# Operands of single-pass float32 matmuls moved to fixed places within 512 bytes of on-chip memory

## The chip, the cores and the metric

One core of one Trainium2 chip runs the whole kernel as one program. The metric is device time in microseconds, the median of several executions. TensorE (PE) multiplies: for each matmul it first loads a 128x128 block of weights (an instruction of its own, PEld in the profile) and then streams the columns of the other operand, the moving one, past it. VectorE (DVE), ScalarE (ACT) and GpSimd (POOL) do the rest, SyncE (SP) issues most transfers. On-chip memory has 128 partitions; an operand of a matmul lies at one byte address, the same in all partitions.

## The reference

Three parts in a row, on 8 sequences of 3072 tokens of width 256, in float32.

```
X = rfft(x, axis=1)
Yr = Xr @ w_r - Xi @ w_i + b_r;  Yi = Xr @ w_i + Xi @ w_r + b_i
Yr, Yi = sign(Y) * max(|Y| - 0.01, 0)        # each
x = irfft(Yr + i Yi)                         # 24576 x 256
# experts, top 1 of 8, where x @ w_skip > 0:
x = x + gate * (relu(x @ w1[e]) @ w2[e])     # 256 -> 1024 -> 256
# feed forward
h = max(x @ w1, x @ w2, x @ w3);  out = h @ w_out   # 256 -> 768 -> 256
```

## The kernel before

To keep float32's accuracy with single-pass matmuls (the type `fp32r`), the kernel splits an operand in two: a high part (ACT's copy into `fp32r`) and a low part (the rest, by DVE or POOL), and sums three products: high by high, high by low and low by high. So each product of the three parts is a group of three matmuls, or of a multiple of three. Some small products of the Fourier steps are plain `fp32`, which the profile shows as two passes each.

**Spectral stage** (`spectral`), one batch after the other, the order written out by hand. The Fourier transform is done in two steps forward (`f1_mm`, L264; `f2`, L281) and two back (`if2`, L345; `if1`, L359). In between `wmm` (L316) multiplies by `w_r` and `w_i`: its weights (the operand that stays in PE) are the data, `xh` and `xl` from pool `fst`, its moving operands the split matrices `wrh`, `wrl`, `wih`, `wil`. For a batch there are 12 steps with two frequency groups each: 8 passes of L281, 24 matmuls of L316, 6 of L345 (11 of the 12 steps). In L345 the constants `ic2h`, `ic2l` are the weights and `yh`, `yl` move. Then `to_rows` (L370) brings the tokens back into rows and multiplies by the gate, and `gating` writes each token to a row of its expert by an indirect DMA.

**Expert stage** (`experts`): a loop over tiles of 256 tokens of one expert, 52 of them here. In an iteration 48 matmuls of L910 make the hidden layer (weights `w1h`, `w1l`, moving `xh`, `xl`, 256 columns) and 48 of L933 the output (weights `hh`, `hl`, moving `w2h`, `w2l`, 256 columns). The tiles' table (`hot`, `q`, `tab`) is worked out on DVE ahead of the loop from `grid`, a constant that counts up, which is loaded at the kernel's start and kept.

**Feed-forward stage** (`feed_forward`): 24 blocks of 1024 tokens, nine units each; a unit is one of three weight matrices at one of three column pairs, as a Strassen-like product of seven half-size products (`product`, L1048: weights `wu`, moving `xh`, `xl`, 512 columns, three matmuls each). After each third unit the outputs of an earlier one (`outputs`, L1126: weights `wo`, moving `hh`, `hl`, 512 columns) are dealt into the units, four matmuls at a time. Products go to PSUM tiles `pa`, `pb`, `pc`; ACT copies some (`keep`, L1055), DVE adds others (`add`, L1058), takes the maximum (L1093, L1094) and prepares the next block (`prepare`, L986 to L1007). `pb` and `pc` have one buffer each, so the next product into `pb` waits for DVE's addition to have read the last.

**Where tiles lie.** A pool (`tc.tile_pool`) is a stretch of memory. Left-hand pools are stacked upwards in the order in which they are opened, right-hand ones (`side="right"`) downwards from the end, and each tile takes the next bytes in its pool in the order of its first request, rounded up to 32. `keep` is the first left-hand pool; the first pool of each stage (`fcst`, `mcst`, `wst`) begins where it ends. On the right lie the constants and `g2` of the spectral stage (`fec`), its input (`fx`), and after the last batch the feed-forward stage's weights (`fw`).

Of the kernel before, what the change touches and what calls it, by code (L numbers as in the profile page):

```python
# [10 lines left out]
F32 = mybir.dt.float32  # L11
F32R = mybir.dt.float32r
# [10 lines left out]
E = 8  # L23
FF = 1024
F2D = 768
LAM = 0.01
TM = 256
# [3 lines left out]
NBLK = S // 128  # L31
NTMAX = NT // TM + E + 2
WO = 9 * 7 * 128
WL = WO + 6 * 256
WHY = "every count is bounded by the number of tokens"


# [75 lines left out]
@with_exitstack  # L113
def kernel(ctx: ExitStack, tc: tile.TileContext, ins, out: bass.AP):
    nc = tc.nc
    G = E + 1

    dram = ctx.enter_context(tc.tile_pool(name="dram", bufs=1, space=bass.MemoryType.DRAM))
    rows = dram.tile([E * CAP, RW], F32, name="rows")
    xt = dram.tile([NT, D], F32, name="xt")  # L120
    wsc = dram.tile([2, 128, WL], F32, name="wsc")

    keep = ctx.enter_context(tc.tile_pool(name="keep", bufs=1))
    ident = keep.tile([128, 128], F32, name="ident")
    make_identity(nc, ident)
    base = keep.tile([128, G], F32, name="base")
    small = keep.tile([128, 64], F32, name="small")
    nc.sync.dma_start(out=small, in_=ins["c_small"])

    def split(src, h, l, act=True):  # L130
        if act:
            nc.scalar.activation(out=h, in_=src, func=AF.Copy)
        else:
            nc.vector.tensor_copy(out=h, in_=src)
        nc.vector.tensor_tensor(out=l, in0=src, in1=h.bitcast(F32), op=ALU.subtract)

    grid = keep.tile([E, NTMAX], F32, name="grid")
    nc.gpsimd.dma_start(out=grid, in_=ins["c_tile"])

    fw = {}  # L140

    def feed_weights():
        pool = ctx.enter_context(tc.tile_pool(name="fw", bufs=1, side="right", reuse_waits="tile"))
        fw["pool"] = pool
        fw["wo"] = [pool.tile([128, 6, D], F32R, name=f"wo{i}") for i in range(2)]
        for i in range(2):
            nc.sync.dma_start(
                out=fw["wo"][i].rearrange("p c d -> p (c d)").bitcast(F32), in_=wsc[i, :, WO:WL]
            )
            yield  # L150
        for u in range(2):
            load_unit(u)
            yield

    def load_unit(u):
        t = fw["pool"].tile([128, 2, 896], F32R, tag="wu", name="wu", bufs=3)
        at = 896 * (u % 9)
        nc.sync.dma_start(
            out=t.bitcast(F32), in_=wsc[:, :, at:at + 896].rearrange("w p f -> p w f")
        )  # L160
        fw[u] = t

    spectral(tc, ins, rows, xt, wsc, base, small, ident, split, feed_weights(), G)
    experts(tc, ins, rows, xt, base, small, grid, ident, split, G)
    feed_forward(tc, xt, fw, load_unit, out)


def spectral(tc, ins, rows, xo, wsc, base, small, ident, split, feed, G):
    nc = tc.nc
    x = ins["x"]  # L170
    with ExitStack() as ctx, ExitStack() as early:
        cst = ctx.enter_context(tc.tile_pool(name="fcst", bufs=1))
        ec = early.enter_context(tc.tile_pool(name="fec", bufs=1, side="right"))
        xp = early.enter_context(tc.tile_pool(name="fx", bufs=4, side="right"))
        big = ctx.enter_context(tc.tile_pool(name="fbig", bufs=5))
        zp = ctx.enter_context(tc.tile_pool(name="fz", bufs=3))
        st = ctx.enter_context(tc.tile_pool(name="fst", bufs=2))
        gp = ctx.enter_context(tc.tile_pool(name="fg", bufs=1))
        ps = ctx.enter_context(tc.tile_pool(name="fps", bufs=2, space=bass.MemoryType.PSUM))

        yk = cst.tile([128, NBLK, CW], F32, name="yk")
        f1 = cst.tile([N1, 128], F32, name="f1")
        c2 = ec.tile([128, NF, 128], F32, name="c2")
        ic2h = ec.tile([128, NF, 128], F32R, name="ic2h")
        ic2l = ec.tile([128, NF, 128], F32R, name="ic2l")
        ic2 = ec.tile([128, 2, 128], F32, name="ic2")
        ic1 = cst.tile([128, N1], F32, name="ic1")
        tri = cst.tile([128, 128], F32, name="tri")
        bt = cst.tile([NBLK // 2 * G, 2, (NBLK + 1) * G], F32, name="bt")
# [1 line left out]
        ones = cst.tile([128, 128], F32, name="ones")  # L191
        bias = cst.tile([128, 256], F32, name="bias")
        bias0 = cst.tile([128, 256], F32, name="bias0")
        wrh = cst.tile([128, 2, 256], F32R, name="wrh")
        wrl = cst.tile([128, 2, 256], F32R, name="wrl")
        wih = cst.tile([128, 2, 256], F32R, name="wih")
        wil = cst.tile([128, 2, 256], F32R, name="wil")
        tok = cst.tile([128, NBLK], F32, name="tok")
        pad = yk[:, 0:1, 0:RW]
        nc.gpsimd.memset(pad, 0.0)  # L200
        nc.gpsimd.memset(pad[:, :, 257:258], 1e6)
# [9 lines left out]
        with tc.manual_schedule():  # L211
# [6 lines left out]

            warm(9)
            nc.sync.dma_start(out=f1, in_=ins["c_f1"])  # L220
            wr = st.tile([128, 2, 256], F32, tag="v", name="wr", bufs=1)
            wi = st.tile([128, 2, 256], F32, tag="c", name="wi", bufs=1)

            ic2f = zp.tile([128, 32, 128], F32, tag="z", name="ic2f")

# [6 lines left out]
            xt = load_x(0, range(4))  # L232
            for h, o in enumerate((0, CW - G)):
# [3 lines left out]
                    out=gi[:, o + E:o + G], in_=ins["moe_w_skip"][sl].rearrange("(p o) -> p o", o=1)  # L237
# [345 lines left out]
            g2 = f1_all(0, xt)  # L583
# [14 lines left out]
            for b in range(B):  # L598
                nxt = b + 1 < B
                if b == 0:  # L600
                    for e in range(E):
                        a = nc.sync.dma_start(
                            out=rows[CAP * e:CAP * e + TM].rearrange("(p s) c -> p s c", s=2),
                            in_=pad.to_broadcast([128, 2, RW]),
                        )
                        tc.add_to_no_dep_group("dispatched", a.ins)
                if nxt:
                    xt = load_x(b + 1, range(4))
# [120 lines left out]
                if nxt:  # L729
                    g2 = g2n  # L730
# [1 line left out]
                pass  # L732


def experts(tc, ins, rows, xo, base, small, grid, ident, split, G):
    nc = tc.nc
    w1d, w2d = ins["moe_w1"], ins["moe_w2"]
    with ExitStack() as ctx:
        cst = ctx.enter_context(tc.tile_pool(name="mcst", bufs=1, reuse_waits="tile"))
        st = ctx.enter_context(tc.tile_pool(name="mst", bufs=1, reuse_waits="tile"))  # L740
# [2 lines left out]

        w2h = cst.tile([128, 8, D], F32R, name="w2h")
        w2l = cst.tile([128, 8, D], F32R, name="w2l")
        hh = cst.tile([128, 8, TM], F32R, name="hh")
        hl = cst.tile([128, 8, TM], F32R, name="hl")
        xs = cst.tile([128, 8, 64], F32, name="xs")
        xt = cst.tile([128, 2, TM], F32, name="xt")
        xr = cst.tile([128, 2, RW], F32, name="xr")  # L750
        xh = cst.tile([128, 2, TM], F32R, name="xh")
        xl = cst.tile([128, 2, TM], F32R, name="xl")
        idx = cst.tile([128, 2], I32, name="idx")
        zero = cst.tile([128, 2], I32, name="zero")
        w1f = cst.tile([128, 2, FF], F32, name="w1f")
        w2f = cst.tile([128, 8, D], F32, name="w2f")
        w1h = cst.tile([128, 2, FF], F32R, name="w1h")
        w1l = cst.tile([128, 2, FF], F32R, name="w1l")

        def value(ap, hi, engines=None):  # L760
            kw = {} if engines is None else {"engines": engines}
            return nc.values_load(ap, min_val=0, max_val=hi, skip_runtime_bounds_check_because=WHY, **kw)

# [34 lines left out]
        with tc.manual_schedule():  # L798
# [12 lines left out]
                out=ti, in0=base[0:E, 0:E], scalar=float(TM - 1), in1=at, op0=ALU.add, op1=ALU.subtract  # L811
# [3 lines left out]
            for i, d in enumerate((1, 2, 4)):  # L815
                nc.vector.tensor_tensor(
                    out=sums[:, i + 1, 4:12], in0=sums[:, i, 4:12], in1=sums[:, i, 4 - d:12 - d], op=ALU.add
# [4 lines left out]
                out=most[:, 0, 4:12], in0=sums[:, 3, 3:11], scalar=1.0, in1=has, op0=ALU.add, op1=ALU.mult  # L822
            )
            for i, d in enumerate((1, 2, 4)):
                nc.vector.tensor_tensor(
                    out=most[:, i + 1, 4:12], in0=most[:, i, 4:12], in1=most[:, i, 4 - d:12 - d], op=ALU.max
# [4 lines left out]
                out=has[0:1], in0=most[0:1, 3, 4:12], scalar1=0.0, scalar2=None, op0=ALU.is_equal  # L831
# [10 lines left out]
                out=top, in0=base[0:E, 0:E], scalar1=-float(TM), scalar2=None, op0=ALU.add  # L842
# [4 lines left out]
                out=v, in0=v, in1=ident[0:E, 0:E].unsqueeze(1).to_broadcast([E, 6, E]), op=ALU.mult  # L847
# [11 lines left out]
                out=q[:, 0], in0=grid, scalar1=float(TM), scalar2=o, op0=ALU.mult, op1=ALU.add  # L859
            )  # L860
            nc.vector.scalar_tensor_tensor(
                out=q[:, 0], in0=q[:, 0], scalar=top, in1=hot, op0=ALU.min, op1=ALU.mult
# [3 lines left out]
                out=q[:, 2], in0=grid, scalar1=1.0, scalar2=starts, op0=ALU.add, op1=ALU.is_equal  # L866
# [14 lines left out]
            for j, copy in enumerate((nc.scalar.copy, nc.vector.tensor_copy)):  # L881
                copy(
                    out=v[:, j].rearrange("p k (q c) -> p k q c", q=4),
                    in_=xr[:, j, 0:D].rearrange("p (q k c) -> p k q c", q=4, k=2),
# [7 lines left out]
        with tc.manual_schedule(), tc.For_i(0, nt, 1, iteration_sync="reg_based") as t:  # L892
# [3 lines left out]
            for c in range(4):  # L896
# [8 lines left out]
                for j in range(2):  # L905
                    f0 = 128 * (2 * c + j)
                    i = 0
# [9 lines left out]
                    out=hl[:, sl], in0=p, scalar=0.0, in1=hh[:, sl].bitcast(F32), op0=ALU.max, op1=ALU.subtract  # L917
# [10 lines left out]
            for j in range(2):  # L928
                y = py.tile([128, D], F32, name="y_ps")
                i = 0  # L930
                for c in range(8):
                    for a, v in ((hh, w2h), (hl, w2h), (hh, w2l)):
# [5 lines left out]
                    out=ob[:, j], in0=y, scalar=xr[:, j, 256:257], in1=xr[:, j, 0:256],  # L938
# [3 lines left out]
                    out=seen[:, j], in0=ob[:, j, 0:1], in1=ob[:, j, 1:2], op=ALU.add  # L942
# [3 lines left out]
                        out=xo[:, :],  # L946
                        out_offset=bass.IndirectOffsetOnAxis(ap=idx[:, j:j + 1], axis=0),
                        in_=ob[:, j],
# [285 lines left out]
```

## Time and profile before

| | us |
|---|---|
| median of 3 runs | 2979.63 (2975.47 to 2982.6) |
| the profiled execution's own time | 2972.22 |
| its span, first to last instruction | 2970.5 |
| mean granted clock of TensorE | 0.987 |

The span is shorter than the execution's time by what lies around it. The profile's busy times say how long an engine had something in it; matmuls overlap, so that the sum of their durations says little, and the starts in the timeline say how many a stretch took. [...] Times in the timeline are from the span's start.

### The profile page before, as it was taken

Reading aid. Unit: us, or ns where it says so; the run is one execution under the profiler, and the core shown is the slowest. Engines: PE = TensorE matmul, PEld = TensorE weight load, DVE = VectorE, ACT = ScalarE, POOL = GpSimd, SP = SyncE. Lnnn points to the kernel's source line nnn. Section 1 sums busy time; section 2 is a strip of 40 time slices with the busy share of each in tenths; the row PEclk is TensorE's granted clock in tenths of the full one; section 3 lists DMA queues with packets and bytes.
Section 4 is the critical chain, followed back from the end, with each engine's and each line's share of the span. In section 5 each row is a group of like instructions: output and inputs, shape, how many; then the busy total and the mean of one; then the engine's idle time right before and its main releaser. Section 6 shows DMA issues by size and latency. Waiting matters only on the chain.

```text
span 2970.5 us, 53442 instructions
## 1 busy us (share of the span) xinstructions
PE 2876.5 (97%) x17158; PEld 2492.8 (84%) x17159; DVE 1835.7 (62%) x2707; ACT 1374.1 (46%) x2657; POOL 1224.4 (41%) x1206
## 2 busy tenths in 40 slices
PE   9999999999969999999699999999999999999998
PEld 8889988898969999999577777777777777777776
DVE  6877777766545455544466665666656666666664
ACT  4444544454423333333255555555555555555553
POOL 2033223222432222222255555555555555555554
PEclk9999999999979999999899999999999999999999
DMA  5323333332343333333356555665556655566543
GB/s 154 123 89 106 103 108 93 110 98 89 102 131 103 96 100 102 94 103 93 92 161 179 165 163 157 177 179 165 163 157 177 179 165 163 157 177 179 165 149 105
DMA packets 400157, 398.83 MB, mean 134 GB/s; under 512 B 272634, under 2 KB 318279, under 8 KB 399988
## 3 DMA queue, kind: packets, MB, share of 16 engines
q1 hardware_dynamic: 385428, 369.80, 44.4%
q0 software_dynamic: 14560, 26.86, 2.6%
q8 instruction: 97, 1.59, 0.2%
q14 instruction: 72, 0.59, 0.1%
HBM read 307.69 MB, written 101.91 MB: 138 GB/s over the span
## 4 chain that ended last, share of the span: by engine, by line
PE 45%; DVE 3%; ACT 1%; issue 1%; DMA 0%; SPq 0%; POOL 0%; DVEq 0%
PE pa L1048 19%; PE o_ps L1126 12%; PE pb L1048 10%; PE pc L1048 5%; DVE m L1094 2%; ACT hh L1105 1%; DVE xl L1007 1%; DVE m L1058 0%; ACT xh L1004 0%; DVE xc L986 0%; DMA xs<-xt 0%; SPq L980 0%; POOL hl L1106 0%; DVE xt L991 0%; DVE t L1058 0%
## 5 line engine op out<-in xcount | busy, mean ns | idle before, releaser
L1048 PE MATMUL pa<-xh,wu 128*128 128x512 f32 x1728 | 616.4, 397 | 19.9 <-ACT xh L1004 19.6
L1055 ACT ACTIVATE s<-pa 128x512 f32<-128x512 f32 x648 | 379.2, 596 | 338.1 <-PE pa L1048 215.1
L1106 POOL TENSOR_TENSOR hl<-m,hh 128x512 fp32r<-128x512 f32 x288 | 398.3, 1405 | 301.5 <-ACT hh L1105 301.5
L1048 PEld LDWEIGHTS pa<-xh,wu 128*128 128x128 f32 x1728 | 325.8, 189 | 99.9 <-ACT xh L1004 19.8
L1048 PE MATMUL pb<-xh,wu 128*128 128x512 f32 x864 | 347.9, 403 | 7.6 <-DVE m L1058 5.9
L1048 PE MATMUL pa<-xl,wu 128*128 128x512 f32 x864 | 342.8, 397 | 3.5 <-DVE xl L1007 3.5
L1126 PE MATMUL o_ps<-hh,wo 128*128 128x512 f32 x1152 | 340.7, 398 | 3.4 <-ACT hh L1105 3.4
L1085 POOL TENSOR_TENSOR t<-s,s 128x512 f32<-128x512 f32 x144 | 186.9, 1298 | 268.3 <-ACT s L1055 268.3
L1126 PEld LDWEIGHTS o_ps<-hh,wo 128*128 128x128 f32 x1152 | 217.5, 189 | 57.3 <-ACT hh L1105 4.7
L915 ACT ACTIVATE hh<-h_ps 128x512 fp32r<-128x512 f32 x208 | 120.6, 597 | 299.5 <-PE h_ps L910 283.7
L1055 ACT ACTIVATE s<-pb 128x512 f32<-128x512 f32 x216 | 129.4, 599 | 272.2 <-PE pb L1048 272.0
L1094 DVE TENSOR_TENSOR m<-m,t 128x1536 f32<-128x1536 f32 x144 | 251.8, 1748 | 0.0
L916 DVE SCALAR_TENSOR_TENSOR hl<-h_ps,hh 128x512 fp32r<-128x512 f32 x208 | 139.4, 689 | 174.6 <-ACT hh L915 143.0
L933 PE MATMUL y_ps<-w2l,hh 128*128 128x256 f32 x832 | 236.2, 284 | 1.0 <-POOL w2l L778 0.4
L933 PE MATMUL y_ps<-w2h,hl 128*128 128x256 f32 x832 | 235.4, 283 | 0.0
L933 PE MATMUL y_ps<-w2h,hh 128*128 128x256 f32 x832 | 235.3, 283 | 0.0
L469 POOL DMA_INDIRECT rows<-yk,pos x192 | 195.3, 1017 | 91.9 <-issue 60.9
L910 PE MATMUL h_ps<-xh,w1h 128*128 128x256 f32 x832 | 230.1, 277 | 1.6 <-DVEq L892 1.6
L910 PE MATMUL h_ps<-xl,w1h 128*128 128x256 f32 x832 | 230.1, 277 | 0.0
L910 PE MATMUL h_ps<-xh,w1l 128*128 128x256 f32 x832 | 229.8, 276 | 0.0
L1048 PEld LDWEIGHTS pb<-xh,wu 128*128 128x128 f32 x864 | 162.8, 188 | 65.2 <-DVE m L1058 15.9
L1105 ACT ACTIVATE hh<-m 128x512 fp32r<-128x512 f32 x288 | 165.7, 626 | 81.4 <-DVE m L1094 81.4
(248 smaller groups left out, 6989.2 us busy)
## 6 DMA issues: line engine op xcount, KB each, us to landing
wu<-wsc SPq DMA_DIRECT2D x216, 896.0 KB
xc<-in_x_dram SPq DMA_DIRECT2D x64, 384.0 KB
xt<-yk SPq DMA_DIRECT2D x192, 128.0 KB
xs<-xt SPq DMA_DIRECT2D x192, 128.0 KB
out_dram<-ob SPq DMA_DIRECT2D x192, 128.0 KB
xr<-rows SPq DMA_DIRECT2D x53, 264.0 KB
xs<-rows SPq DMA_DIRECT2D x208, 64.0 KB, 2.3
w1f<-in_moe_w_dram SPq DMA_DIRECT2D x9, 1024.0 KB
```

What stands on the lines that cost most here:

```text
L469: a = nc.gpsimd.indirect_dma_start(out=rows[:, :], out_offset=bass.IndirectOffsetOnAxis(ap=pos, axis=0), in_=yk[:, t, G:G + RW], in_offset ...
L910: nc.tensor.matmul(p[:, j], lhsT=a[:, k, f0:f0 + 128], rhs=v[:, k], start=(i == 0), stop=(i == 5))
L915: nc.scalar.activation(out=hh[:, sl], in_=p, func=AF.Relu)
L916: nc.vector.scalar_tensor_tensor(out=hl[:, sl], in0=p, scalar=0.0, in1=hh[:, sl].bitcast(F32), op0=ALU.max, op1=ALU.subtract)
L933: nc.tensor.matmul(y, lhsT=a[:, c, 128 * j:128 * j + 128], rhs=v[:, c], start=(i == 0), stop=(i == 23))
L1048: nc.tensor.matmul(o, lhsT=self.w[:, g, at:at + 128], rhs=v[h], start=(start and i == 0), stop=(i == 2), skip_group_check=True,)
L1055: nc.scalar.activation(out=self.s[k], in_=o, func=AF.Copy)
L1085: nc.gpsimd.tensor_tensor(out=self.t[:, 2], in0=self.s[5], in1=self.s[7], op=ALU.add)
L1094: nc.vector.tensor_tensor(out=m[:, 0:3], in0=m[:, 0:3], in1=self.t, op=ALU.max)
L1105: nc.scalar.activation(out=hh[:, i], in_=m[:, i], func=AF.Copy)
L1106: nc.gpsimd.tensor_tensor(out=hl[:, i], in0=m[:, i], in1=hh[:, i].bitcast(F32), op=ALU.subtract)
L1126: nc.tensor.matmul(o, lhsT=wo[g][:, 2 * p + c, 128 * k:128 * k + 128], rhs=h[v][:, (0, 3, 1, 2)[2 * t + c]], start=(p == 0 and i == 0), st ...
```

## The change

Nothing that is computed, no order of matmuls and no shape is changed; tiles are requested in another order, unused tiles (`spacer`) are put between, and one constant moves from one pool to another. `spacer(pool, n)` requests n float32 values per partition, 4n bytes, that nobody uses.

```diff
+def spacer(pool, n, i=0):
+    pool.tile([128, n], F32, name=f"spacer{i}", bufs=1)
...
-    grid = keep.tile([E, NTMAX], F32, name="grid")
-    nc.gpsimd.dma_start(out=grid, in_=ins["c_tile"])
...
     (feed_weights, after wo0, wo1 and the first two wu)
+        spacer(pool, 120)
...
     (spectral)
+        st = ctx.enter_context(tc.tile_pool(name="fst", bufs=2))
         big = ctx.enter_context(tc.tile_pool(name="fbig", bufs=5))
         zp = ctx.enter_context(tc.tile_pool(name="fz", bufs=3))
-        st = ctx.enter_context(tc.tile_pool(name="fst", bufs=2))
...
+        wrh = cst.tile([128, 2, 256], F32R, name="wrh")
+        wrl, wih, wil likewise, now the first tiles of cst
         yk = cst.tile([128, NBLK, CW], F32, name="yk")
...
+        ec.tile([128, 16, 256, 2], F32, tag="g2", name="g2")
+        spacer(ec, 120)
...
-        tok = cst.tile([128, NBLK], F32, name="tok")
+        tok = gp.tile([128, NBLK], F32, name="tok")
...
+            spacer(st, 16)
             wr = st.tile([128, 2, 256], F32, tag="v", name="wr", bufs=1)
             wi = st.tile([128, 2, 256], F32, tag="c", name="wi", bufs=1)
+            for t in ("yh", "yl"):
+                st.tile([128, 2, 256], F32R, tag=t, name=t, bufs=1)
+            spacer(st, 16, 1)
...
     (experts)
         w2h = cst.tile([128, 8, D], F32R, name="w2h")
         w2l = cst.tile([128, 8, D], F32R, name="w2l")
+        xh = cst.tile([128, 2, TM], F32R, name="xh")
+        xl = cst.tile([128, 2, TM], F32R, name="xl")
+        spacer(cst, 16)
         hh = cst.tile([128, 8, TM], F32R, name="hh")
         hl = cst.tile([128, 8, TM], F32R, name="hl")
+        w1h = cst.tile([128, 2, FF], F32R, name="w1h")
+        w1l = cst.tile([128, 2, FF], F32R, name="w1l")
         xs = cst.tile([128, 8, 64], F32, name="xs")
         xt = cst.tile([128, 2, TM], F32, name="xt")
         xr = cst.tile([128, 2, RW], F32, name="xr")
-        xh, xl, and further down w1h, w1l from their old places
...
+        grid = cst.tile([E, NTMAX], F32, name="grid")
+        nc.sync.dma_start(out=grid, in_=ins["c_tile"])
```

## Rows read from the trace of the kernel before

**Rows 1.** The page, part 1: engine, busy us, share of the span, instructions.
```profile
PE 2876.5 (97%) x17158; PEld 2492.8 (84%) x17159; DVE 1835.7 (62%) x2707; ACT 1374.1 (46%) x2657; POOL 1224.4 (41%) x1206
```

**Rows 2.** Windows by stage: stretch, its length, busy us (instructions) per engine, clock, DMA.
```profile
0.00:856.00 856.00, 806.20 (x5902) 731.51 (x5903) 607.44 (x1115) 398.01 (x945) 245.53 (x330) 0.97 0.35 108
856.00:1442.00 586.00, 584.89 (x4991) 583.53 (x4992) 291.80 (x511) 185.64 (x320) 156.10 (x273) 1.00 0.35 99
...
1462.00:2970.00 1508.00, 1484.98 (x6264) 1177.53 (x6264) 934.72 (x1078) 789.79 (x1391) 820.39 (x600) 0.99 0.59 164
```

**Rows 3.** Waits of the feed-forward stage: engine, line, releaser; us, times, longest.
```profile
PEld pb L1048 <- DVE m L1058: 15.9, 23, 0.7
PEld pb L1048 <- DVE t L1058: 11.8, 25, 1.4
```

**Rows 4.** Timeline of PE, one expert iteration (start us, us); then the page, part 5.
```profile
1104.24 0.28 PE L910 MATMUL h_ps<-xh,w1h 128*128 128x256 f32 x1
...
1108.00 0.28 PE L910 MATMUL h_ps<-xh,w1h 128*128 128x256 f32 x1
...
1109.70 0.28 PE L933 MATMUL y_ps<-w2h,hh 128*128 128x256 f32 x1
...
1115.45 0.28 PE L910 MATMUL h_ps<-xh,w1h 128*128 128x256 f32 x1
...
L933 PE MATMUL y_ps<-w2l,hh 128*128 128x256 f32 x832 | 236.2, 284 | 1.0 <-POOL w2l L778 0.4
```

**Rows 5.** Groups of weight loads, shapes apart: busy us, mean ns.
```profile
L933 PEld LDWEIGHTS y_ps<-w2h,hh 128*128 128x128 f32 x832 | 159.5, 192 | 0.0
L910 PEld LDWEIGHTS h_ps<-xh,w1h 128*128 128x128 f32 x832 | 156.4, 188 | 1.9 <-ACT xh L132 1.9
```

**Rows 6.** Timeline of PE, one step of the spectral stage.
```profile
266.75 0.28 PE L316 MATMUL bankC<-wrh,xl 128*128 128x256 f32 x1
...
269.36 0.28 PE L345 MATMUL bankD<-yh,ic2h 128*128 128x256 f32 x1
...
270.07 1.10 PE L281 MATMUL bankB<-c,g 128*128 128x128 f32 x8
```

**Rows 7.** Timeline of PE, feed-forward stage without a wait; windows of that stretch.
```profile
2877.72 0.40 PE L1048 MATMUL pb<-xl,wu 128*128 128x512 f32 x1
...
2952.22 0.40 PE L1048 MATMUL pa<-xh,wu 128*128 128x512 f32 x1
...
2877.71:2952.21 74.50, 74.50 (x319) 1.00 0.42 125
```

**Rows 8.** Timeline of PE at the cold start; windows of that stretch.
```profile
1470.57 0.63 PE L1048 MATMUL pb<-xh,wu 128*128 128x512 f32 x1
...
1471.42 0.63 PE L1048 MATMUL pb<-xh,wu 128*128 128x512 f32 x1
...
1470.57:1471.42 0.85, 0.85 (x3) 0.50 0.07 19
```

**Rows 9.** Timeline of DVE, then of PE, at one stall.
```profile
2005.37 0.69 DVE L1093 TENSOR_TENSOR m<-pa,m 128x512 f32<-128x512 f32 x1 [0.88 <-PE pa L1048]
...
2010.24 0.68 DVE L1058 TENSOR_TENSOR m<-pb,s 128x512 f32<-128x512 f32 x1
...
2010.97 0.50 PE L1048 MATMUL pb<-xh,wu 128*128 128x512 f32 x1 [0.26 <-DVE m L1058]
```

**Rows 10.** Timeline of SP's queue and of DVE at the stage change; the page, part 6.
```profile
817.71 14.00 SPq L375 DMA_DIRECT2D xt<-yk  x9
844.91 0.40 SPq L765 DMA_DIRECT2D w1f<-in_moe_w_dram  x1
...
845.45 0.26 DVE L856 TENSOR_SCALAR hot<-grid,own 8x106 f32<-8x106 f32 x1
...
xs<-rows SPq DMA_DIRECT2D x208, 64.0 KB, 2.3
```

More of the change, by code (lines that the diff above doesn't have):

```diff
@@ L163 @@
     spectral(tc, ins, rows, xt, wsc, base, small, ident, split, feed_weights(), G)
-    experts(tc, ins, rows, xt, base, small, grid, ident, split, G)
+    experts(tc, ins, rows, xt, base, small, ident, split, G)
     feed_forward(tc, xt, fw, load_unit, out)
@@ L174, in spectral @@
         xp = early.enter_context(tc.tile_pool(name="fx", bufs=4, side="right"))
+        st = ctx.enter_context(tc.tile_pool(name="fst", bufs=2))
         big = ctx.enter_context(tc.tile_pool(name="fbig", bufs=5))
         zp = ctx.enter_context(tc.tile_pool(name="fz", bufs=3))
-        st = ctx.enter_context(tc.tile_pool(name="fst", bufs=2))
         gp = ctx.enter_context(tc.tile_pool(name="fg", bufs=1))
         ps = ctx.enter_context(tc.tile_pool(name="fps", bufs=2, space=bass.MemoryType.PSUM))
+        wrh = cst.tile([128, 2, 256], F32R, name="wrh")
+        wrl = cst.tile([128, 2, 256], F32R, name="wrl")
+        wih = cst.tile([128, 2, 256], F32R, name="wih")
+        wil = cst.tile([128, 2, 256], F32R, name="wil")
         yk = cst.tile([128, NBLK, CW], F32, name="yk")
@@ L193, in spectral @@
         bias0 = cst.tile([128, 256], F32, name="bias0")
[L194 to L197, printed above, removed]
-        tok = cst.tile([128, NBLK], F32, name="tok")
+        tok = gp.tile([128, NBLK], F32, name="tok")
         pad = yk[:, 0:1, 0:RW]
@@ L732, in spectral, with experts @@
                 pass
-def experts(tc, ins, rows, xo, base, small, grid, ident, split, G):
+def experts(tc, ins, rows, xo, base, small, ident, split, G):
     nc = tc.nc
@@ L750, in experts @@
         xr = cst.tile([128, 2, RW], F32, name="xr")
-        xh = cst.tile([128, 2, TM], F32R, name="xh")
-        xl = cst.tile([128, 2, TM], F32R, name="xl")
         idx = cst.tile([128, 2], I32, name="idx")
@@ L756, in experts @@
         w2f = cst.tile([128, 8, D], F32, name="w2f")
-        w1h = cst.tile([128, 2, FF], F32R, name="w1h")
-        w1l = cst.tile([128, 2, FF], F32R, name="w1l")
+        grid = cst.tile([E, NTMAX], F32, name="grid")
+        nc.sync.dma_start(out=grid, in_=ins["c_tile"])
         def value(ap, hi, engines=None):
```

## The prediction

> **What bounds the kernel now.** I read the page's part 1 first: PE is busy 97% of the span [rows 1]. Then the busy time by stage: the spectral stage (0 to 856 us), the expert loop (856 to 1442) and the feed-forward stage (1462 to 2970) have PE busy for 806, 585 and 1485 us at 0.97 to 1.00 of the clock, and no other engine is above 71% of a stage [rows 2]. Then who PE waits for: in the feed-forward stage its weight loads wait 48 times for `pb` (23 for DVE's `m`, 25 for DVE's `t`), 27.7 us together, and little else [rows 3]. So what PE needs from one matmul's start to the next, its interval, is the time of the kernel, and I read it from start times in the timeline. A matmul's own duration is no use here, since neighbours overlap.
>
> The change only moves operands, so the question is whether an interval depends on where its operands lie. Positions follow from the order of allocation (each tile rounded up to 32 bytes). Before, the pools behind `keep` begin at 384 within 512 bytes; the diff takes the 424-byte `grid` out of `keep`, so they begin at 448, and 64 bytes of `spacer` lead from 448 to 0. 480 bytes of `spacer` in the right-hand pools, which end at 480, bring their tiles from 480 to 0. Weights / moving operands, before and after, within 512 bytes:
> - L910 (`w1h`, `w1l` / `xh`, `xl`): 0 / 448, and the same after.
> - L933 (`hh`, `hl` / `w2h`, `w2l`): 384 / 384, after 0 / 448.
> - L316 (`xh`, `xl` / `wrh` to `wil`): 160 and 416 / 320, after 0 and 256 / 448, since a row of `xh` is 768 bytes and every second one lies 256 further on.
> - L345 (`ic2h`, `ic2l` / `yh`, `yl`): 480 / 416, after 0 / 448.
> - L1048 and L1126 (`wu`, `wo` / `xh`, `xl`, `hh`, `hl`): 480 / 384, after 0 / 448.
>
> So L910 is already where all are to go, and the kernel before holds its own experiment: two products of equal shape (128x128 weights, 256 columns), side by side in one loop at full clock. L910's 48 intervals from 1104.24 to 1109.70 are 113.8 ns each, the last 15, from 1108.00 on, 113.3; L933's 48 from 1109.70 to 1115.45 are 5.75 us, 119.8 ns [rows 4]. L933's weight loads are longer too, 192 against 188 ns [rows 5]. L316's 22 intervals from 266.75 to 269.36 are 118.6 ns each, L345's six to 270.07 118.3 [rows 6]. In the feed-forward stage 318 matmuls of 512 columns from 2877.72 to 2952.22 take 234.3 ns each, all beside a clock of 1.00 [rows 7]. [...]
>
> **The change part by part.**
>
> Experts, L933. 2,496 matmuls (three groups of 832 [rows 4]) go from 119.8 to L910's 113.3, 6.5 ns each: 16.2 us. What must keep up is the next tile's `xl` (L135), in an iteration that gets 48 x 6.5 ns = 0.3 us shorter; it isn't late now, since PE waits for nothing in this stage (584.9 busy of 586) [rows 2]. This is the surest term; below nothing isn't excluded, since its operands differ from L910's in more than place (bounds 0 to 16).
>
> Spectral, L316 and L345. L316 has 2,304 matmuls (24 in each of 12 steps of 8 batches). Of them 64 have `x0` as weights, which lies in `yl`'s place at 448 and gains nothing, and 96 are first of their group behind a wait. For some 2,150, 118.6 to 113.8 (L910 with its few slower intervals behind the switch), 4.8 ns: 10.3 us. L345's 528 (3 products, 2 frequencies, 11 steps, 8 batches): 4.5 ns, 2.4 us. DVE is the next engine at 71% [rows 2], so I take 12 of these 12.7. If the half of L316's weights at 256 were no better than L933, 6 less; bounds 0 and 13.
>
> The fp32 products of this stage (L264, L281, L359, L370) are moved too. Nothing in the trace prices that; if L933 against L910 is the nearest, 2,560 passes of L281, L359 and L370 times 6.5 ns are 17 us either way. I take 0: L281's pair keeps its relation (480 / 480, after 0 / 0), and for the others no row gives a sign.
>
> Feed-forward, L1048 and L1126: 6,264 matmuls [rows 2]; less the cold start, the stalls and the tail, some 6,100. This is the term that decides, and no row has 512 columns at 0 / 448. The bounds: 213.3 (the cold intervals halved) and, on the other side, twice L933's loss, 213.3 + 26.2 = 239.5. Between them I choose by shape. The loss before goes with the columns: 21.0 in 512 at 480 / 384, about 12 in 256 at the similarly spaced 416 / 320 of L316. [...] So I scale L910's 6.6 to twice the columns: 213.3 + 13.3 = 226.6, nearest to the row of exactly this placement. Saved: 7.7 ns x 6,100 = 47 us.
>
> Not all of it comes through. At the 48 stalls [rows 3] PE waits for a DVE chain: L1093 starts at 2005.37 when PE's `pa` is done, four more operations follow, and with L1058's read of `pb` from 2010.24 the next `pb` can start at 2010.97 [rows 9]. That is 5.6 us, 24 intervals of PE's, and the chain doesn't get shorter: each stall grows by 24 x 7.7 ns = 0.18 us, 9 us together. Net 38 us. Bounds: 32 us slower at 239.5 ns, 104 faster at 213.3 (128, less 24 at the stalls).
>
> `grid`. Its load leaves the Pool queue at the start, where nothing waits for it, and stands in SP's queue behind the spectral stage's last `xt` store. It must wait for the z tile that lay in its place, whose last reader is an L370 matmul; behind it SP has only L765. SP's last nine stores are issued from 817.71 for 14.00 us, L765 goes out at 844.91, and the first reader of `grid` (L856) starts at 845.45 [rows 10]. In these 13 us a small load lands (a 64 KB one takes 2.3 us [rows 10]). Cost 0; uncovered 2.3 us.
>
> Sum against the profiled execution (2972.2 us, span 2970.5): 16 + 12 + 38 = 66 us, 2906. The median of the runs is 2979.6, 7.4 above it, so 2913.
>
> [...] L910 and L933 have equal shapes and differ by 6.5 ns [rows 4]. [...]
>
> **The rivals.**
> - *More comes back.* L910's 6.6 ns may be a cost per matmul, not per column. Then 512 columns take 213.3 + 6.6 = 219.9, saving 14.4 x 6,100 = 88, less 48 x 24 x 14.4 ns = 17 at the stalls: 71 + 28 = 99 us, 2881. [...]
> - *512 columns don't gain.* The loss of the longer matmul comes from its own stream, and 234.3 stays: 28 us, 2952. [...] Against: L910 streams as fast and loses at most 6.6 per 256.
> - *Placement isn't the cause*, or what decides isn't the place within 512 bytes: L933 differs from L910 in its tensors and its PSUM pool. Then nothing moves: 2980. [...]
> - *Slower.* 0 / 448 suits 256 columns and not 512: the stream passes the bytes of the loading weights once more in the second half, and each matmul takes up to 239.5 ns. +5.2 x 6,100 = 32 against 28 gained: 2984. It decides from 234.3 + 28 / 6.1 = 238.9 ns on. For it: no row shows 512 columns there. [...]
>
> **How the numbers follow.** Forecast 0.42, more 0.25, 512 columns don't gain 0.18, placement isn't the cause 0.07, slower 0.08. The range reaches below 2881 for an interval of 216 ns, near the columns' own time (112 - 21 + 28 = 119 us, 2861) and above 2952 for that rival without the spectral term (2964). The forecast's own range, 222 to 231 ns with the spectral bounds, is 2890 to 2942. With 0.2% (6 us) about what can be told from no change: faster 0.85 (the first three), same 0.08, slower 0.07.
>
> **What would show it.** L933's intervals at 113.3 ns and its weight loads at 188; L316 and L345 near 113.8; L1048 and L1126 at 226.6 (219.9, 234.3 and 239.5 are the rivals); the 48 waits for `pb` grown from 28 to some 37 us; L856 not waiting for `grid`. Wrong it is if L933 stays at 119.8, or if the intervals shrink and the span doesn't.

## The result and the profile after

The changed kernel takes 2951.58 us (median of 4 runs, 2949.81 to 2956.84) against 2979.61 (2975.47 to 2982.6) before: ratio 0.991, 95% interval 0.9892 to 0.9927, 28 us less. 66 us less, 2913, was the forecast. The profiled execution takes 2949.81 us, its span is 2948.1, and the clock is 0.987 as before.

The stages of the changed kernel in the windows view (stretch, its length, then busy us and instructions of PE, PEld, DVE, ACT and POOL, clock, DMA share, GB/s). The boundaries are the ends of the stages; the third stretch is the passage between the last two:

```profile
0.00:852.48 852.48, 802.38 (x5903) 726.56 (x5904) 607.68 (x1115) 397.84 (x945) 244.46 (x329) 0.98 0.35 109
852.48:1422.96 570.48, 570.21 (x4992) 568.90 (x4992) 288.54 (x511) 187.01 (x320) 154.59 (x273) 1.00 0.37 101
1422.96:1442.01 19.05, 0.16 (x2) 0.00 (x1) 1.79 (x3) 0.63 (x1) 2.20 (x3) 0.59 0.37 66
1442.01:2948.00 1505.99, 1481.35 (x6264) 1176.20 (x6264) 936.63 (x1078) 789.67 (x1391) 820.34 (x600) 0.99 0.62 164
```

The stretches of [rows 2] were rounded, so I took each stage between the same instructions in both traces. The spectral stage takes 851.4 us (before 855.0), the experts 570.4 (585.9), the feed-forward 1499.1 (1502.1). Of the 22.4 us that the span lost, 15.5 come from the experts, and 3.6 and 3.0 from the stages in which 12 and 38 were forecast. These are single executions: the first matmul of the expert loop starts at 840.3 and at 844.8 us in two of the runs below (`ex_only`, `ff_only`) that leave the spectral tiles where they were, so 3.6 us by themselves would tell little.

The intervals show why. First an expert iteration in the timeline of PE (start us, us, then the instruction), the answer to [rows 4]:

```profile
1106.15 0.28 PE L921 MATMUL h_ps<-xh,w1h 128*128 128x256 f32 x1
...
1111.59 0.28 PE L944 MATMUL y_ps<-w2h,hh 128*128 128x256 f32 x1
...
1117.03 0.28 PE L921 MATMUL h_ps<-xh,w1h 128*128 128x256 f32 x1
```

and the weight loads of `y_ps` in the groups with shapes apart (busy us, mean ns), the answer to [rows 5]:

```profile
L944 PEld LDWEIGHTS y_ps<-w2h,hh 128*128 128x128 f32 x832 | 156.2, 188 | 0.0
```

L944 (L933 before) now takes 5.44 us for 48 matmuls, 113.3 ns each, exactly as long as L921 (L910 before); its loads take 188 ns.

Next two steps of the spectral stage, the answer to [rows 6]. Both run from the second matmul of L324 (L316 before) to the first of L353 (L345 before), 23 intervals; the row ahead of each is what PE did just before the step:

```profile
136.08 0.60 PE L427 MATMUL bankA<-ones,gm 128*108 128x128 f32 x4
...
136.64 0.28 PE L324 MATMUL bankC<-wrl,xh 128*128 128x256 f32 x1
...
139.26 0.28 PE L353 MATMUL bankD<-yh,ic2h 128*128 128x256 f32 x1
...
159.24 1.10 PE L289 MATMUL bankB<-c,g 128*128 128x128 f32 x8
...
160.29 0.28 PE L324 MATMUL bankC<-wrl,xh 128*128 128x256 f32 x1
...
163.00 0.28 PE L353 MATMUL bankD<-yh,ic2h 128*128 128x256 f32 x1
```

The first takes 113.9 ns an interval, the second 117.8, with the same operands at the same places within 512 bytes. Of the 96 such steps 15 are of the first kind (113.3 to 114.3) and 75 of the second (117.7 to 118.4); in the other six, each the first of a batch, L324 also waits. The mean over L324 is 117.1 (L316 118.5 before), over L353 116.9 (L345 116.8 before; intervals without a wait). Which kind a step is isn't chance: all 14 steps directly behind a matmul of `gating` (L427 or L438) are of the first, the fourth and fifth step of each batch from the second batch on, and of the 76 others without a wait all but one are of the second. That the matmuls ahead of a step are the cause isn't shown: no run changes them and nothing else.

Last, the feed-forward stage, the answer to [rows 7]: a stretch without a wait in the timeline of PE, the same stretch in the windows of PE (busy us and instructions, clock, DMA share, GB/s), and, for [rows 3], the waits for `pb` (us in total, times, longest):

```profile
2793.48 0.40 PE L1059 MATMUL pb<-xl,wu 128*128 128x512 f32 x1
...
2847.14 0.40 PE L1059 MATMUL pc<-xh,wu 128*128 128x512 f32 x1
```

```profile
2793.47:2847.13 53.66, 53.66 (x231) 1.00 0.53 157
```

```profile
PEld pb L1059 <- DVE m L1069: 16.5, 24, 0.7
PEld pb L1059 <- DVE t L1069: 10.9, 24, 1.2
```

230 intervals in 53.66 us are 233.3 ns each, where 226.6 was forecast and 234.3 stood before. The waits of the weight loads stay at 27.4 us (27.7 before): with 1 ns gained, nothing to speak of is given back there.

### The profile page after: what moved, and what is told of

It is laid out like the page before. It is cut to its first block, busy times and chain, and to the rows that moved or that the text cites. A ratio compares the mean times of both kernels' runs of the same rounds, so it can differ in the third digit from the quotient of the medians.

```text
span 2948.1 us, 52560 instructions
## 1 busy us (share of the span) xinstructions
PE 2854.1 (97%) x17158; PEld 2471.7 (84%) x17159; DVE 1834.6 (62%) x2707; ACT 1375.1 (47%) x2657; POOL 1221.6 (41%) x1205
## 4 chain that ended last, share of the span: by engine, by line
PE 45%; DVE 3%; ACT 1%; issue 1%; DMA 0%; SPq 0%; POOL 0%; DVEq 0%
PE pa L1059 19%; PE o_ps L1137 12%; PE pb L1059 10%; PE pc L1059 5%; DVE m L1105 2%; ACT hh L1116 1%; DVE xl L1018 1%; DVE m L1069 0%; ACT xh L1015 0%; DVE xc L997 0%; DMA xs<-xt 0%; SPq L991 0%; POOL hl L1117 0%; DVE xt L1002 0%; DVE m L1104 0%
## 5 line engine op out<-in xcount | busy, mean ns | idle before, releaser
L921 PE MATMUL h_ps<-xh,w1h 128*128 128x256 f32 x832 | 230.4, 277 | 1.6 <-DVEq L903 1.6
L944 PE MATMUL y_ps<-w2h,hl 128*128 128x256 f32 x832 | 230.6, 277 | 0.3 <-DVE hl L927 0.3
L921 PE MATMUL h_ps<-xh,w1l 128*128 128x256 f32 x832 | 230.5, 277 | 0.0
L944 PE MATMUL y_ps<-w2l,hh 128*128 128x256 f32 x832 | 230.5, 277 | 0.0
L921 PE MATMUL h_ps<-xl,w1h 128*128 128x256 f32 x832 | 230.4, 277 | 0.0
L944 PE MATMUL y_ps<-w2h,hh 128*128 128x256 f32 x832 | 229.7, 276 | 0.0
```

The source lines that it names most:

```text
L921: nc.tensor.matmul(p[:, j], lhsT=a[:, k, f0:f0 + 128], rhs=v[:, k], start=(i == 0), stop=(i == 5))
L944: nc.tensor.matmul(y, lhsT=a[:, c, 128 * j:128 * j + 128], rhs=v[:, c], start=(i == 0), stop=(i == 23))
```

## The experiments

The kernel before ran again beside each set of runs: 2979.61 us above, 2960.69 beside the first four kernels here, 2958.53 beside the last four. Across sets only ratios are compared. The two sweeps are single executions.

My theory after this result: the place of the operands does set the interval, but a longer matmul doesn't scale like a shorter one. The rivals: 512 columns take 234 ns wherever they lie; or something else in the feed-forward stage (DMA, DVE, longer waits) holds them up.

**The three parts, one at a time.** Each kernel moves the operands of one stage to 0 / 448 and leaves the other two where they were. The lines that matter:

```diff
 ex_only (kernel before, with the experts' new order of tiles)
-    grid = keep.tile([E, NTMAX], F32, name="grid")
+    spacer(keep, NTMAX)
 ff_only (kernel before, feed-forward tiles brought to 0 / 448)
+        spacer(pool, 120)
+        spacer(st, 16)
 sp_only (changed kernel, the two later stages put back)
+        spacer(cst, 112)
+        spacer(st, 112)
-        spacer(pool, 120)
```

> The expert stage's tiles at 0 / 448, all others where they were. All theories: L933's matmuls at 113.3 ns instead of 119.9, 2,496 of them, 16 us faster than before (ratio 0.9945); nothing else moves.

> The feed-forward stage's tiles at 0 / 448, all others where they were. Theory A: intervals of 233.3 instead of 234.3 ns, 6 us over 6,264 matmuls less what the waits for pb take back, 3 to 6 us (ratio 0.998 to 0.999). The rival, that the stage gained more and the other stages lost it again: 10 us or more (0.9965 or less).

> The spectral stage's tiles as after the change (grid loaded late as there), the experts' and the feed-forward stage's where they were. Profile of the change: that stage 3.6 us shorter, so ratio 0.9988; the rival is that the 28 us of the medians against 22.7 of the two profiled executions lie here, 8 us or more (0.9973 or less).

Measured: experts alone 0.9943 (0.9929 to 0.9956, 2943.76 us against 2960.69, 16.9 us less), feed-forward alone 0.9981 (0.9972 to 0.999, 4.5 us less), spectral alone 0.9985 (0.9976 to 0.9994, 4.9 us less). Together 26.3 us of the whole change's 28, within the intervals: the parts add up, and nothing to speak of is lost between them. (`grid` is loaded late in the first and the third, as in the changed kernel.)

The expert loop of `ex_only` holds something that I had not expected. Two of its iterations in the timeline of PE:

```profile
1135.22 0.28 PE L917 MATMUL h_ps<-xh,w1h 128*128 128x256 f32 x1
...
1140.66 0.28 PE L940 MATMUL y_ps<-w2h,hh 128*128 128x256 f32 x1
...
1157.83 0.28 PE L917 MATMUL h_ps<-xh,w1h 128*128 128x256 f32 x1
...
1163.48 0.28 PE L940 MATMUL y_ps<-w2h,hh 128*128 128x256 f32 x1
```

The 48 intervals of the first are 113.3 ns each, those of the second 117.7, with the same tiles at the same places. Of the 52 iterations 11 are of the second kind, in two stretches, each of which begins at a change of the expert's weights. The loop takes 572.7 us here and 570.4 in the changed kernel. So the two values of the spectral stage turn up in this stage too.

**A sweep of places without the rest of the kernel.** Groups of 30 equal matmuls, one behind the other; a group's interval is the next group's start less its own, divided by 30. Weights at 0 and moving operands at 32 k in groups a (512 columns) and b (256), the letter behind the underline counting k from a; weights at 32 k and moving at 448 in group c; 128 + 32 k columns at 0 / 448 in group d. The columns' time, over which a loss is counted, is an estimate: half of what the columns take at a granted clock of 0.50. There L324 of the changed kernel takes 213.3 ns for 256 columns (12 intervals from 225.50 to 228.06 us, clock 0.50 in the windows), so it is 106.7 ns for 256, 213.3 for 512, and in proportion for the others.

```diff
+        for r in range(30):
+            a = wt[r % len(wt)] // 4
+            nc.tensor.matmul(p[0:cols, 0:n], lhsT=w[:, a:a + cols], rhs=m[:, mv // 4:mv // 4 + n])
```

> Leaves out the whole computation: only groups of 30 fp32r matmuls back to back, with nothing else running, at places that are swept (its output means nothing). Theory A, the loss is the stream's own: 512 columns take about 233 ns at weights 0 / moving 448 and much the same at every other moving place; with 128 to 512 columns the loss over the columns' time grows in steps, about 6.7 ns for each further 128 columns (113.3 at 256, 173.3 at 384, 233.3 at 512); loads of 32, 64 or 96 weight columns change nothing. Theory B, 0 / 448 is the place for 256 columns and another one is for 512: some of the 16 moving places or 15 weight places has 512 columns at 226.7 ns or less. Theory C, the loss comes from the weight load beside the stream: a load of 32 weight columns loses about a quarter of the 20 ns, 218 to 220 ns, and the step from 256 to 512 columns costs only the columns' time. For 256 columns all three: 113.3 at 0 / 448, about 120 at 0 / 0, and weights at 256 with moving 448 tell why L324 (L316 before) stayed near 117: 113.3 if only the place within 256 bytes counts, more if that within 512 does.

Its timeline of PE (start us, us of the group, then the instruction), of which each pair of rows gives an interval; then its windows over all groups:

```profile
42.14 6.96 PE L141 MATMUL a_a<-m,w 128*128 128x512 f32 x30
48.94 7.16 PE L141 MATMUL a_b<-m,w 128*128 128x512 f32 x30
...
76.81 7.19 PE L141 MATMUL a_f<-m,w 128*128 128x512 f32 x30
83.84 7.17 PE L141 MATMUL a_g<-m,w 128*128 128x512 f32 x30
...
97.84 6.99 PE L141 MATMUL a_i<-m,w 128*128 128x512 f32 x30
104.66 7.16 PE L141 MATMUL a_j<-m,w 128*128 128x512 f32 x30
...
139.56 7.17 PE L141 MATMUL a_o<-m,w 128*128 128x512 f32 x30
146.57 7.16 PE L141 MATMUL a_p<-m,w 128*128 128x512 f32 x30
153.56 3.76 PE L141 MATMUL b_a<-m,w 128*128 128x256 f32 x30
157.16 3.70 PE L141 MATMUL b_b<-m,w 128*128 128x256 f32 x30
...
203.22 3.60 PE L141 MATMUL b_o<-m,w 128*128 128x256 f32 x30
206.65 3.71 PE L141 MATMUL b_p<-m,w 128*128 128x256 f32 x30
...
307.81 7.00 PE L141 MATMUL c_o<-m,w 128*128 128x512 f32 x30
314.65 7.15 PE L141 MATMUL c_p<-m,w 128*128 128x512 f32 x30
...
331.67 3.52 PE L141 MATMUL d_d<-m,w 128*128 128x224 f32 x30
335.03 3.59 PE L141 MATMUL d_e<-m,w 128*128 128x256 f32 x30
...
42.14:430.00 387.86, 387.86 (x2070) 330.25 (x2069) 0.00 (x0) 0.00 (x0) 0.00 (x0) 1.00 0.00 1
```

512 columns at 0 / 448 (a_o) take 233.7 ns here too, with DVE, ACT and POOL idle and a DMA share of 0.00 (the last row): the rest of the stage isn't the cause. But at 0 / 0 (a_a) they take 226.7, at 0 / 256 (a_i) 227.3 and at 448 / 448 (c_o) 228.0, while 0 / 160 (a_f), the relation that the feed-forward stage had before, takes 234.3. With 256 columns it is the reverse: 0 / 448 (b_o) takes 114.3 and 0 / 0 (b_a) 120.0. (Such a pair takes in the change to the next group and a group's first matmuls, up to 1.3 ns an interval more; starts inside the groups give 113.3, 226.7 and 233.3, and the numbers below are of that kind where no rows are named.) Group d, at 0 / 448, takes 113.3 ns at 256 columns, 146.7 at 320, 174.8 at 384, 202.2 at 448 and 233.4 at 512: over the columns' time 6.6, 13.3, 14.8, 15.5 and 20.1 ns, a loss that doesn't go in proportion to the columns. Below 256 columns the interval hardly shrinks any more: 110 to 112 ns at 128, 160, 192 and 224 (d_d, 224 columns: 112.0). So at 256 columns something other than the columns may already set the interval, and its 6.6 ns is no measure of a loss per column. Three more suspects fall. Weights at 256 instead of 0, or at both in turn, leave 256 columns under 448 at 113.3 ns, so the second of L324's two places isn't what keeps most of its steps at 117.8. Loads of 32, 64 and 96 weight columns instead of 128 leave 231.8, 232.8 and 228.2 ns at 0 / 448, so the load's length explains at most part of it; four pieces of 128 columns, 1024 bytes apart, take 226.7 from 0 and 233.3 from 448, so how often the stream crosses a multiple of 512 bytes makes no difference here.

**All places against all.** 8 x 8 places in steps of 32 bytes, for 512 columns (groups p) and 256 (groups q), weights by the first letter and moving operands by the second; then 256 to 512 columns in steps of 32 at distance 0 (r) and at 160 (s). Distance is the moving operand's place less the weights', modulo 256.

```diff
+            run(bank("p", 8 * i + j), [32 * i], 32 * j, 512)
```

> Leaves out the whole computation, as the first sweep: groups of 30 matmuls for all 8 x 8 places of weights and moving operand within 256 bytes in steps of 32, with 512 and with 256 columns, then 256 to 512 columns at distance 0 and at 160. Theory R, only the distance of the moving operand from the weights within 256 bytes decides: along each diagonal one interval, for 512 columns 226.7 at distance 0, 229 at 64, 233 to 234.3 else; for 256 columns 120 at 0, 113.3 at 192, 117 to 120 else. Rival, the places themselves count too (a place that is no multiple of 64): diagonals that differ by 2 ns or more. And: the loss is one of each matmul (13 ns, changed by place) and not of its columns: at distance 0, 13 ns over the columns' time at every number of columns; a loss by columns would go from 6.7 to 13 or from 13 to 26 between 256 and 512.

Its timeline of PE for 512 columns, weights 0 and moving at 0 and 160 (pa_a, pa_f), both 32 bytes on (pb_b, pb_g), and two of the 256-column groups at distance 192 (qa_g at 0 / 192, qd_b at 96 / 32); then its windows over all groups:

```profile
41.34 6.96 PE L141 MATMUL pa_a<-m,w 128*128 128x512 f32 x30
48.14 7.16 PE L141 MATMUL pa_b<-m,w 128*128 128x512 f32 x30
...
76.02 7.19 PE L141 MATMUL pa_f<-m,w 128*128 128x512 f32 x30
83.04 7.17 PE L141 MATMUL pa_g<-m,w 128*128 128x512 f32 x30
...
104.04 6.99 PE L141 MATMUL pb_b<-m,w 128*128 128x512 f32 x30
110.86 7.16 PE L141 MATMUL pb_c<-m,w 128*128 128x512 f32 x30
...
138.74 7.19 PE L141 MATMUL pb_g<-m,w 128*128 128x512 f32 x30
145.76 7.17 PE L141 MATMUL pb_h<-m,w 128*128 128x512 f32 x30
...
508.36 3.60 PE L141 MATMUL qa_g<-m,w 128*128 128x256 f32 x30
511.79 3.71 PE L141 MATMUL qa_h<-m,w 128*128 128x256 f32 x30
...
575.61 3.69 PE L141 MATMUL qd_b<-m,w 128*128 128x256 f32 x30
579.14 3.71 PE L141 MATMUL qd_c<-m,w 128*128 128x256 f32 x30
...
41.34:801.00 759.66, 759.66 (x4351) 670.43 (x4350) 0.00 (x0) 0.00 (x0) 0.00 (x0) 1.00 0.00 1
```

The last row says that PE never stopped, at a clock of 1.00, with no other engine busy. For 512 columns every one of the eight distances has one interval, to about 1 ns, wherever the pair lies (pa_a 226.7 and pb_b 227.3, pa_f and pb_g 234.0):

| distance | 0 | 32 | 64 | 96 | 128 | 160 | 192 | 224 |
|---|---|---|---|---|---|---|---|---|
| 512 columns, ns | 226.7 | 233.2 | 228.9 | 233.3 | 233.5 | 234.3 | 233.3 | 233.3 |

For 256 columns distance 0 takes 119.5 to 120.0 in all eight, the others 117 to 120, and distance 192 takes 113.3 in five pairs (qa_g) and 117.8 in three (qd_b): the two values of the spectral stage, without that stage. At distance 0 the loss is 13.3 ns in 256 columns, 12 in 288, 13.3 in 320, 352 and 384 (146.7, 160.0, 173.3 ns), 15 to 17 in 416 to 480 (188.4, 202.9, 216.6) and 13.3 again in 512, so my expectation of 13 ns at every number of columns holds only in part. At distance 160 it is 12 in 256, 13 to 14 in 288 to 416, 20 in 448, 17 in 480 and 21 in 512: the 12 and 21 from which the prediction read a loss that goes with the columns are the two ends of a course in steps.

**What follows, in the kernel.** If the distance decides, the feed-forward stage wants 0 where the others want 192. Three kernels: the changed one with its feed-forward weights at 448 under moving operands at 448 (distance 0), the same with weights at 384 (distance 64), and the kernel before with one line added that brings the weights from 480 to 384 under moving operands at 384 (distance 0):

```diff
 best (changed kernel)
-        spacer(pool, 120)
+        spacer(pool, 8)
 after64 (changed kernel)
-        spacer(pool, 120)
+        spacer(pool, 24)
 before_rel0 (kernel before, behind the feed-forward weights)
+        pool.tile([128, 24], F32, name="spacer")
```

> The changed kernel with the feed-forward weights at 448 instead of 0, so that weights and moving operands of 512 columns lie at equal places. Theory R: intervals of 226.7 instead of 233.3 ns; 6.65 ns over some 6,130 matmuls is 41 us, less 8 to 9 at the waits for pb: 32 to 41 us below the changed kernel, ratio to the kernel before 0.977 to 0.980. Theory A (the stream's own loss): no difference to the changed kernel, 0.991.

> The changed kernel with the feed-forward weights at 384, moving operands 64 bytes behind them. Theory R: 228.9 ns, 4.4 below 233.3: 27 us less 5 at the waits, ratio to the kernel before 0.981 to 0.984, between the changed kernel and the one with equal places. Rival: 0.991 as the changed kernel.

> The kernel before with one line more: 96 bytes behind the feed-forward weights, which brings them from 480 to 384, the place of the moving operands; nothing lies at 0 or 448 for that. Theory R: 226.7 instead of 234.3 ns in the feed-forward stage, 47 us less 9 at the waits: 38 to 47 us, ratio 0.984 to 0.987, more than the whole change gave. Rival, 0 / 448 matters as such: about 0.998, as that stage's part of the change gave.

| kernel | us (before: 2958.53) | ratio, 95% interval | feed-forward stage, us | interval, ns |
|---|---|---|---|---|
| best | 2906.88 | 0.9824 (0.981 to 0.9837) | 1468.3 | 227.1 |
| after64 | 2913.85 | 0.9856 (0.9841 to 0.9871) | 1477.9 | 229.0 |
| before_rel0 | 2922.94 | 0.9884 (0.9869 to 0.9899) | 1468.6 | 227.1 |

The first of them over a like stretch of 230 intervals in the timeline of PE, in the windows of PE, and in its waits:

```profile
2632.22 0.40 PE L1059 MATMUL pb<-xl,wu 128*128 128x512 f32 x1
...
2684.43 0.39 PE L1059 MATMUL pc<-xh,wu 128*128 128x512 f32 x1
```

```profile
2632.21:2684.42 52.21, 52.21 (x231) 1.00 0.67 168
```

```profile
PEld pb L1059 <- DVE m L1069: 19.3, 24, 0.8
PEld pb L1059 <- DVE t L1069: 14.2, 24, 1.3
```

52.21 us for 230 intervals are 227.0 ns. All three kernels' intervals come out as in the sweep (226.7, 228.9, 226.7). The times fall a little short of what was expected: 51.7 us gained at distance 0 where 0.977 to 0.980 meant 59 to 68, 44.7 at distance 64 where 0.981 to 0.984 meant 47 to 56, and 35.6 from the one line in the kernel before where 0.984 to 0.987 meant 38 to 47. Some of what an interval gains goes into the waits for `pb`, which grew from 27.4 to 33.5 us in the rows above.

## Why the prediction was wrong

- **PE's interval is the time of the kernel, and the place of its operands sets it: right.** The rival that placement isn't the cause falls by the experts' 15.5 us and by the sweep: at the clock of 1.00 groups with the same number of columns differ, by up to 7.6 ns per 512 columns (234.3 at distance 160, 226.7 at 0). At 0.50 the distances taken don't: 512 columns take 425 ns at distance 160 [rows 8] and 427 at 192 (changed kernel, four intervals from 1454.07 to 1455.78 us), and 256 take 213.3 at both (L316, six intervals from 225.48 to 226.76 us, and the L324 named above).
- **Experts, 16 us: right.** 119.8 to 113.3 ns, 15.5 us in the profile and 16.9 alone. What I read as "384 / 384 against 0 / 448" is distance 0 against distance 192. That 113.3 held in all iterations was not sure: in `ex_only` 11 of 52 took 117.8 at this distance.
- **Feed-forward, 38 us: this step failed.** "So I scale L910's 6.6 to twice the columns: 213.3 + 13.3 = 226.6, nearest to the row of exactly this placement." No run shows the 213.3 for 512 columns, nor the 6.6 and 13.3, which are counted over it and its half: it is half the cold interval, an estimate, and the lowest interval of 512 columns in any run is 226.7. At 0 / 448 they take 233.3 ns in the kernel and in the sweep, 1.0 less than before; the profile shows 5.9 us of intervals, less 3.0 by which the stage's time beyond unstalled intervals grew (its length less 6,263 of them: 34.8 to 37.8 us, while the waits for `pb` stayed), and 4.5 came when this part ran alone. The loss depends on distance and number of columns together, and 192, the best distance for 256 columns, is one of five within 1.1 ns of the worst for 512. I took one shape's best place for a property of the place. The stage's loads are busy 1176.2 us in 6,264 of them, 188 ns of each interval of 233 and so more than half of it. That distance 0 takes 226.7, the number forecast, is coincidence; I hadn't considered it because L933 with its 256 columns is slowest there.
- **Spectral, 12 us: mis-sized, 3.6 in the profile, 4.9 alone.** L316 went from distance 160 to 192, but only 15 of 96 steps settled near 113.9 ns and 75 at 117.8: 118.5 to 117.1 in the mean, some 1.3 ns where 4.8 was forecast. L345 went from 480 / 416 to 0 / 448: both are distance 192. By my list of places it moved; by what counts it didn't (116.8 and 116.9 in the mean), and its 2.4 us had no ground. Its 118.3 at distance 192 was in [rows 6] and spoke against L910's 113.3 as a rule; I didn't see it, since I looked at places and not at distances. (The matmuls with `x0` are 48, not 64, which changes nothing here.) The plain fp32 products, put at 0, stayed: L281 116.6 and 116.7 ns a pass, L359 115.9 both times, L370 119.7 both times.
- **The stalls: right in kind.** The waits for `pb` grow only where the interval shrinks. In before_rel0, whose interval went from 234.3 to 227.1, they went from 27.7 to 35.1 us, and the stage's time beyond unstalled intervals from 34.8 to 46.3: 11.5 where I had set down 9 for 226.6.
- **`grid`, 0: right.** Its load goes out at 831.78, L776 behind it at 842.12, and no reader waits for it.
- **The rivals.** "512 columns don't gain" gave 2952, and 2951.6 came, but its reason falls: the loss isn't in the stream's own nature, since distance 0 takes 7 ns of it away (226.7 against 234.3). It also counted 12 us for the spectral stage, of which 4 to 5 came, and nothing for the feed-forward stage, where 4.5 came; that its number fits so closely is luck. The slower one (239.5 ns) shows at no place. "A cost per matmul, not per column" fits distance 0, where the loss is 13.3 ns for 256 and for 512 columns alike, but not 192 (6.6 and 20.1) nor 160 (12 and 21), and its 219.9 ns is reached nowhere.
- **The range: its upper end is off.** The forecast's own range to 2942 counts 6 us for the spectral stage; with the lower bound of 0 that I gave it, it ends at 2947.

Still open: what in the memory or the engine makes the loss go by the distance modulo 256, and what settles a run at 113.3 or 117.8 ns at one distance, beyond what stands ahead of it in the spectral stage. No run here was made to tell these apart.

## What to carry to other kernels

Before moving operands, list the relation of each pair (moving less weights) beside its measured interval, not the places: two pairs at one distance and with different intervals, as L910 and L345 here, say that the rule isn't understood yet. A cost measured at one shape holds at that shape (0 / 448 lost 6.6 ns over the columns' time in 256 columns and 20.1 in 512); a group of 30 matmuls per shape and distance, without the rest of the kernel, costs one run and gives the interval to about 1 ns where it has one value; 256 columns at distance 192 have two. Where one engine is busy 97% of the span, one spacer of a hundred bytes at the right distance can be worth as much as the whole re-ordering or more (ratio 0.9884 against 0.991).

## What was not expected of the hardware

With a weight load for every matmul and at a clock of 1.00, fp32r took 226.7 to 234.3 ns per 512 columns in the sweeps and 113.3 to 120.0 per 256, by the distance; at no distance did it reach the columns' time, by the estimate 213.3 and 106.7. The distance counted modulo 256 bytes (226.7 at 0 / 0, 227.3 at 0 / 256). At one distance a run of equal matmuls settled at either of two intervals and kept it: 113.3 or 117.8 ns, in the sweep, the spectral stage and the expert loop alike; and 128 to 224 columns at 0 / 448 took 110 to 112 ns, little less than the 113.3 of 256. One trap of the view: from 26 to 32 us the windows show a clock of 1.00 for the sweep's first matmuls of 512 columns, which start 427 ns apart (from 26.42 to 28.56 us), like the 425 at 0.50 in [rows 8]; there the intervals tell the speed and the view doesn't.
